# The order of the first ten loads on one queue: projection weights ahead of the tokens

## The chip, the cores and the metric

The kernel runs on one core of one Trainium2 chip. The metric is the device time of one execution in microseconds (us), the median of several executions; lower is better. Five engines run their own instruction streams side by side: PE (matrix products), ACT (ScalarE), DVE (VectorE), POOL (GpSimd) and SP (SyncE), which here issues every transfer. Transfers run on 16 DMA engines that are fed from one queue.

## The reference

The inputs are 2048 tokens `x` of 448 features, the weights `wqkv` (448 x 1344), `wo`, an MLP (`w1`, `b1`, `w2`, `b2`, hidden size 1792) and a gate vector. Two branches are mixed per token:

```
qkv = x @ wqkv                         # 16 heads of 28
o   = softmax(q . k[t - 2 j], j = 0..7) . v[t - 2 j]     # 8 earlier tokens, two apart, masked below 0
a   = o @ wo
b   = relu(x @ w1 + b1)**2 @ w2 + b2
g   = sigmoid(x . gate_w)
out = g * a + (1 - g) * b
```

All inputs are float32.

## The kernel before, in words

Each float32 operand is split into two parts, a high part (a rounded copy, made by ACT: `activation(..., Copy)` into a tile of type float32r) and a low part (the rest, made by DVE: `tensor_sub(raw, high)`). Each product is then three matmuls: high with high, high with low, low with high. PE has nearly all of the work, and everything else is laid beside it.

The 2048 tokens are four chunks of 512 (`CH`), transposed beforehand on the host so that features lie on partitions. The 448 features make four row tiles: `k` = 0, 1, 2 of 128 rows and `k` = 3 of 64 rows, which is stored twice so that it fills 128 partitions. The weights `wqkv` lie in the same row tiles, three blocks of 448 columns (query, key, value); the query block carries two more columns for the gate (450 columns, `NQ`).

The program opens with 13 matmuls on zeros (line 628) and then loads the first chunk and the query weights, which is the part that the change touches (lines 631 to 640). `raws[0]` is the raw query weight tile (`wqraw` in the profile), `rx` the raw tokens of chunk 0 (`xraw`). SP issues in this order, one DMA each, all on the same queue:

| place | before | KB | line |
|---|---|---|---|
| 1 | weights, row tile 0 (w0) | 225 | L635 |
| 2 | tokens, row tile 0, columns 0 to 255 (x0a) | 128 | L640 |
| 3 | tokens, row tile 0, columns 256 to 511 (x0b) | 128 | L640 |
| 4 | weights, row tile 1 (w1) | 225 | L635 |
| 5 | tokens, row tile 1 (x1) | 256 | L640 |
| 6 | weights, row tile 2 (w2) | 225 | L635 |
| 7 | tokens, row tile 2 (x2) | 256 | L640 |
| 8, 9 | weights, row tile 3, two halves of 64 rows (w3a, w3b) | 112.5 each | L638 |
| 10 | tokens, row tile 3 (x3) | 256 | L640 |

Behind them on the queue come the key and value weights (L645, six loads, and L648) and the tokens of chunk 1 (L561, one load of 1024 KB, which reuses the buffer of the query weights).

The splits follow in the loop over `k` from line 650. For each row tile ACT makes the high part of the weights (L651, `wqh`) and then of the tokens in two halves of 256 columns (L658; the very first half is made by DVE, L656). DVE makes the low parts (L659 weights, L661 tokens). ACT and DVE work strictly in program order, so a copy that waits for its load holds back all copies behind it. Row tile 3 is split at L113 and L114 (`w7h`, `w7l`), and so are the key and value weights.

PE's first real work is `qkv_first` (line 249): for `k` = 0, 1, 2 it runs twelve matmuls of 450 columns (L258): four token tiles of 128, three products each, first the two token tiles of columns 0 to 255, then those of 256 to 511. Then row tile 3 and the key weights follow as pairs of matmuls over 64 rows (L187). From there to the end PE works through the other chunks, the MLP (`h` and `b`) and the output projection (`a`). The order on every engine is written out by hand with a planned clock (`advance`, `at`, `when`), which the change does not touch.

Of the kernel before, what the change touches and what calls it, by code (L numbers as in the profile page):

```python
# [14 lines left out]
P = 128  # L15
# [7 lines left out]
CH = 512  # L23
NQ = D + 2
# [32 lines left out]
def gated_mix_kernel(ctx: ExitStack, tc: tile.TileContext, xT, wqkv, w1, w2, wo, b1, b2, out):  # L57
    nc = tc.nc
# [436 lines left out]
    def raw_tile(name):  # L495
        return rawp.tile([P, 4, 512], F32, tag="raw", name=name)
# [133 lines left out]

    raws = [raw_tile("wqraw0")]
    rx = raw_tile("xraw0")
    for k in range(4):
        if k < 3:
            nc.sync.dma_start(raws[0][:, k, :NQ], wqkv[0, :, k])  # L635
        else:
            for b, rows in ((0, slice(0, 64)), (1, slice(64, P))):
                nc.sync.dma_start(raws[0][rows, k, :NQ], wqkv[b, rows, k])  # L638
        for cols in ((slice(0, 256), slice(256, CH)) if k == 0 else (slice(0, CH),)):
            nc.sync.dma_start(rx[:, k, cols], xT[0, :, k, cols])  # L640

    for b, tag in ((1, "k"), (2, "v")):
        raw = attp.tile([P, 3, D], F32, tag=tag, name=f"wqraw{b}")
# [525 lines left out]
```

## Time and profile before

| | |
|---|---|
| time, median of 3 executions | 414.52 us (414.49 to 414.63) |
| the profiled execution's own time | 414.51 us |
| its span in the profile | 412.7 us |
| PE busy in the span | 408.2 us (99%) |
| DVE, ACT, POOL busy | 255.7, 211.3, 268.5 us |
| moved by DMA | 73.76 MB |

All starts are counted in us from the start of the span; 1.8 us of the execution's own time lie outside the span. A timeline row has the start, the time from there to the end of the last instruction in the row, the engine, the line, the operation, what it writes and reads, and in square brackets how long the engine was idle before and what ended that. "SPq" is a DMA being issued, not being moved. "DMA to landing" counts from the issue.

### The profile page before, as it was taken

What the parts mean: (1) busy time and instruction counts of PE and PEld (TensorE: products, weight loads), DVE (VectorE), ACT (ScalarE), POOL (GpSimd) and SP (SyncE); (2) the same over time, 40 slices, a digit from 0 to 9 for tenths busy, and PEclk for the clock granted to TensorE, in tenths of its full rate; (3) what the DMA queues carried; (4) which work ended last, traced back from release to release, by engine and by line L of the source; (5) the groups of instructions that cost most, each with busy time, mean ns of one, the idle gap of its engine ahead of it and who ended that gap; (6) DMA issues with size and microseconds to landing.
All of it is one profiled execution on the core that took longest, in us unless ns stands there. A gap on an engine that the chain in (4) does not pass through costs nothing.

```text
span 412.7 us, 9327 instructions
## 1 busy us (share of the span) xinstructions
PE 408.2 (99%) x3835; PEld 378.0 (92%) x3835; DVE 255.7 (62%) x404; ACT 211.3 (51%) x477; POOL 268.5 (65%) x167
## 2 busy tenths in 40 slices
PE   8999999999999999999999999999999999999997
PEld 7999999999999999888888888989898888888996
DVE  4520433276767766777656798879576677891354
ACT  4641656388765565444565535444653254346540
POOL 0000001955999999989989899999899977940000
DMA  7989999969362315555112649764146630168304
GB/s 226 380 324 326 268 393 299 335 213 311 101 235 104 128 42 218 209 184 152 29 58 95 228 160 270 197 146 149 27 163 186 229 129 2 45 177 132 96 0 180
DMA packets 65611, 73.76 MB, mean 179 GB/s; under 512 B 32352, under 2 KB 58528, under 8 KB 65184
## 3 DMA queue, kind: packets, MB, share of 16 engines
q1 hardware_dynamic: 65568, 73.16, 55.1%
q8 instruction: 30, 0.49, 0.5%
q14 instruction: 13, 0.11, 0.1%
HBM read 45.71 MB, written 28.25 MB: 179 GB/s over the span
## 4 chain that ended last, share of the span: by engine, by line
PE 97%; DMA 1%; SPq 0%; DVE 0%; ACT 0%; issue 0%
PE b L187 33%; PE h L187 32%; PE qkv L187 23%; PE a L187 7%; PE qkv L258 1%; DMA xraw<-xT 1%; PE a L943 1%; PE last L943 0%; SPq L640 0%; SPq L635 0%; DVE bt L822 0%; ACT x L658 0%; PE last L935 0%; PE a L935 0%
## 5 line engine op out<-in xcount | busy, mean ns | idle before, releaser
L334 POOL TENSOR_TENSOR qk<-q,k 128x896 f32<-128x896 f32 x64 | 135.1, 2137 | 84.8 <-DMA k<-k_d 76.4
L341 POOL TENSOR_TENSOR av<-lg,v 128x896 f32<-128x896 f32 x64 | 119.4, 1961 | 6.3 <-DVE lg L335 5.8
L187 PE MATMUL qkv<-wqh,x 64*128 64x448 f32 (+1 forms) x528 | 89.1, 361 | 0.0
L615 DVE TENSOR_TENSOR h<-h,h 128x512 fp32r<-128x512 f32 x56 | 38.4, 688 | 65.9 <-ACT h L618 65.5
L187 PEld LDWEIGHTS qkv<-wqh,x 64*128 64x128 f32 x528 | 72.2, 184 | 0.8
L187 PE MATMUL qkv<-wql,x 64*128 64x448 f32 (+1 forms) x264 | 72.2, 360 | 0.0
L187 PE MATMUL b<-w2ah,h 64*128 64x448 f32 x448 | 68.5, 359 | 0.0
L187 PE MATMUL b<-w2bh,h 64*128 64x448 f32 x448 | 67.8, 360 | 0.0
L335 DVE TENSOR_REDUCE lg<-qk 128x32 f32<-128x896 f32 x64 | 67.0, 1074 | 0.0
L349 DVE TENSOR_REDUCE o<-av 128x112 f32<-128x896 f32 x64 | 66.4, 1070 | 0.1
L616 ACT ACTIVATE h<-h,b1z 128x512 f32<-128x512 f32 x56 | 36.7, 655 | 43.6 <-PE h L187 43.6
L187 PEld LDWEIGHTS b<-w2ah,h 64*128 64x128 f32 x448 | 46.9, 184 | 2.8
L187 PEld LDWEIGHTS b<-w2bh,h 64*128 64x128 f32 x448 | 45.3, 184 | 3.2 <-ACT h L567 0.3
L187 PEld LDWEIGHTS qkv<-wql,x 64*128 64x128 f32 x264 | 44.5, 184 | 0.4
L187 PE MATMUL b<-w2al,h 64*128 64x448 f32 x224 | 44.3, 358 | 0.0
L187 PE MATMUL b<-w2bl,h 64*128 64x448 f32 x224 | 43.2, 358 | 0.0
L206 ACT ACTIVATE st<-qkv 128x448 f32<-128x448 f32 x48 | 24.3, 546 | 34.8 <-PE qkv L187 26.9
L617 ACT ACTIVATE h<-h 128x512 fp32r<-128x512 f32 x56 | 33.5, 598 | 1.7
L618 ACT ACTIVATE h<-h 128x512 f32<-128x512 f32 x56 | 33.3, 594 | 0.0
L187 PE MATMUL h<-x,w1h 64*128 64x512 f32 x168 | 32.8, 386 | 0.0
L567 ACT ACTIVATE h<-h 128x4 fp32r<-128x4 f32 (+1 forms) x35 | 7.2, 207 | 43.1 <-PE b L187 43.0
L187 PE MATMUL h<-x2b,w1h 64*128 64x512 f32 x168 | 28.2, 386 | 0.0
(145 smaller groups left out, 728.7 us busy)
## 6 DMA issues: line engine op xcount, KB each, us to landing
k<-k_d SPq DMA_DIRECT2D x8, 840.0 KB, 6.4
v<-v_d SPq DMA_DIRECT2D x8, 840.0 KB, 4.8
x_d<-x SPq DMA_DIRECT2D x11, 512.0 KB, 6.6
q_d<-st SPq DMA_DIRECT2D x8, 448.0 KB, 4.1
k_d<-st SPq DMA_DIRECT2D x8, 448.0 KB, 4.6
v_d<-st SPq DMA_DIRECT2D x8, 448.0 KB, 5.9
w1raw<-w SPq DMA_DIRECT2D x4, 896.0 KB, 9.2
q<-q_d SPq DMA_DIRECT2D x8, 448.0 KB, 3.6
```

The costliest lines, as they stand in the source:

```text
L187: nc.tensor.matmul(acc.pt[:, :acc.n], a[rows], w[rows], start=acc.todo == acc.all, stop=acc.todo == 1)
L206: nc.scalar.activation(st[:, :, t % 2], pt[:, :D].rearrange("p (g c) -> p g c", g=G), AF.Copy)
L258: nc.tensor.matmul(acc.pt[:, :NQ], a, w, start=k == j == 0, stop=False)
L334: nc.gpsimd.tensor_mul(pr, q[:, s:s + 1].to_broadcast([P, W, C]), k[:, s:s + W])
L335: pending.append(lambda: nc.vector.tensor_reduce(lg[:, s], pr.rearrange("p w (h d) -> p w h d", h=HG), axis=AX.X, op=ALU.add))
L341: nc.gpsimd.tensor_mul(pr.rearrange("p (h d) w -> p w h d", h=HG), lg[:, s][:, :, :, None].to_broadcast([P, W, HG, DH]), v[:, s:s + W].rea ...
L349: nc.vector.tensor_reduce(o[:, g * C:(g + 1) * C], pr, axis=AX.X, op=ALU.add)
L567: nc.scalar.activation(ap, f32(ap), AF.Copy)
L615: nc.vector.tensor_sub(hl, pt, f32(hh))
L616: ops += [lambda pt=pt, r=r: nc.scalar.activation(pt, pt, AF.Relu, bias=b1t[:, f + r:f + r + 1]), lambda pt=pt, hh=hh: nc.scalar.activatio ...
L617: lambda pt=pt, hh=hh: nc.scalar.activation(hh, pt, AF.Square),
L618: lambda pt=pt, r=r, low=low: (nc.scalar.activation(pt, pt, AF.Square), at(delays[r], low))]
```

## The change

The ten loads are put in another order. The weights of each row tile are issued ahead of the (rest of the) tokens of the row tile before it. The sizes of the loads, the tiles they fill, and every instruction of PE, ACT, DVE and POOL and their order stay as they are.

| place | before | after |
|---|---|---|
| 1 | w0 | w0 |
| 2 | x0a | x0a |
| 3 | x0b | w1 |
| 4 | w1 | x0b |
| 5 | x1 | w2 |
| 6 | w2 | x1 |
| 7, 8 | x2, w3a | w3a, w3b |
| 9 | w3b | x2 |
| 10 | x3 | x3 |

```diff
-    for k in range(4):
+    rxf, xf = rx.rearrange("p k n -> p (k n)"), xT[0].rearrange("p k n -> p (k n)")
+
+    def w_raw(k):
         if k < 3:
             nc.sync.dma_start(raws[0][:, k, :NQ], wqkv[0, :, k])
-        else:
-            for b, rows in ((0, slice(0, 64)), (1, slice(64, P))):
-                nc.sync.dma_start(raws[0][rows, k, :NQ], wqkv[b, rows, k])
-        for cols in ((slice(0, 256), slice(256, CH)) if k == 0 else (slice(0, CH),)):
-            nc.sync.dma_start(rx[:, k, cols], xT[0, :, k, cols])
+            return
+        for b, rows in ((0, slice(0, 64)), (1, slice(64, P))):
+            nc.sync.dma_start(raws[0][rows, k, :NQ], wqkv[b, rows, k])
+
+    def x_raw(lo, hi):
+        nc.sync.dma_start(rxf[:, lo:hi], xf[:, lo:hi])
+
+    w_raw(0)
+    x_raw(0, 256)
+    w_raw(1)
+    x_raw(256, 512)
+    w_raw(2)
+    x_raw(512, 1024)
+    w_raw(3)
+    x_raw(1024, 1536)
+    x_raw(1536, 4 * CH)
```

## The prediction

> **What bounds the kernel now.** I read the page first, then the chain of waits, then the timeline of the first 12 us by engine, because the change touches only loads that are issued there.
>
> ```profile
> span 412.7 us, 9327 instructions
> PE 408.2 (99%) x3835; PEld 378.0 (92%) x3835; DVE 255.7 (62%) x404; ACT 211.3 (51%) x477; POOL 268.5 (65%) x167
> PE 97%; DMA 1%; SPq 0%; DVE 0%; ACT 0%; issue 0%
> ```
>
> PE is busy for 408.2 of 412.7 us and makes 97% of the chain that ended last. So the end of the kernel is the moment at which PE can start without a break, plus a fixed amount of PE work. The chain, in order of time, tells where that moment is, and the waits of PE over the whole span whether there is another one:
>
> ```profile
> 2.60 4.59 DMA xraw<-xT
> ...
> 7.22 0.42 ACT x L658
> ...
> 7.69 5.09 PE qkv L258 x24
> 12.78 12.28 PE qkv L187 x117
> ```
>
> ```profile
> PE qkv L258 <- ACT x L658: 0.3, 1, 0.3
> ```
>
> The load issued at 2.60 is x1, the tokens of row tile 1. It lands at 2.60 + 4.59 = 7.19; ACT copies its first half from 7.22 on; PE starts row tile 1 at 7.69 and from there is never short of work. (PE's one wait after its warm-up is shown as 0.3 us because the ends of matmuls are modelled.) From landing to PE it is 7.69 - 7.19 = 0.50 us. Whatever moves x1's landing moves the end by the same amount, in either direction, until another step is later.
>
> How the landings follow one another is seen in ACT's timeline, where a copy that waited begins when its load has landed:
>
> ```profile
> 3.45 0.58 ACT L651 ACTIVATE wqh<-wqraw 128x450 fp32r<-128x450 f32 x1 [1.42 <-DMA wqraw<-wqkv]
> 5.42 0.42 ACT L658 ACTIVATE x<-xraw 128x256 fp32r<-128x256 f32 x1 [1.39 <-DMA xraw<-xT]
> 6.05 0.58 ACT L651 ACTIVATE wqh<-wqraw 128x450 fp32r<-128x450 f32 x1 [0.21 <-DMA wqraw<-wqkv]
> 7.22 0.72 ACT L658 ACTIVATE x<-xraw 128x256 fp32r<-128x256 f32 x2 [0.59 <-DMA xraw<-xT]
> 7.88 0.58 ACT L651 ACTIVATE wqh<-wqraw 128x450 fp32r<-128x450 f32 x1
> 9.22 0.72 ACT L658 ACTIVATE x<-xraw 128x256 fp32r<-128x256 f32 x2 [0.76 <-DMA xraw<-xT]
> 10.04 0.58 ACT L113 ACTIVATE w7h<-wqraw 128x450 fp32r<-128x450 f32 x1
> 10.57 0.63 ACT L113 ACTIVATE x<-xraw 128x512 fp32r<-128x512 f32 x1
> ```
>
> These are w0, x0b, w1, x1, w2, x2, row tile 3 of the weights, x3: the landings come in the order of issue. Before x1's copy ACT sat idle for 0.59 us with w1 already copied. The weights of row tile 1 are therefore not what row tile 1 waits for; its tokens are.
>
> Issue is no limit. SP issues the ten loads by 5.27 + 0.58 us, while most land later than 5:
>
> ```profile
> 2.13 0.43 SPq L635 DMA_DIRECT2D wqraw<-wqkv  x1
> 2.60 0.43 SPq L640 DMA_DIRECT2D xraw<-xT  x1
> 3.08 0.43 SPq L635 DMA_DIRECT2D wqraw<-wqkv  x1
> 3.55 0.43 SPq L640 DMA_DIRECT2D xraw<-xT  x1
> 4.03 1.20 SPq L638 DMA_DIRECT2D wqraw<-wqkv  x2
> 5.27 0.58 SPq L640 DMA_DIRECT2D xraw<-xT  x1
> ```
>
> The busy time by stretches (last two columns: share of the DMA engines, GB/s) says what is the limit:
>
> ```profile
> 3.25:4.25 1.00, 1.00 (x7) 0.91 (x5) 0.48 (x2) 0.58 (x1) 0.00 (x0) 1.00 0.56 117
> 4.25:7.25 3.00, 3.00 (x13) 2.36 (x12) 1.79 (x4) 1.03 (x3) 0.00 (x0) 1.00 1.00 303
> 7.25:10.00 2.75, 2.43 (x12) 2.17 (x12) 1.76 (x5) 1.94 (x5) 0.00 (x0) 1.00 1.00 299
> ```
>
> From 4.25 on the transfers run at some 300 GB/s with all engines busy: the queue is worked off in order and a load lands when the bytes ahead of it are through. Before that there is a dip of about 1 us at 117 GB/s, just behind the first two loads.
>
> **The change part by part.** No instruction of PE, ACT, DVE or POOL changes or changes place; ten loads of the same sizes keep one queue. Only landings move.
>
> *x1 goes from fifth to sixth place; w2 (225 KB) goes ahead of it.* By bytes: 225 x 1024 = 230,400 bytes at 303 GB/s are 0.76 us. By a row: x1 will have ahead of it and in it exactly the set of loads that w2 had before (w0, x0a, x0b, w1, x1, w2). The landing times by line give w2's:
>
> ```profile
> L635 SPq DMA_DIRECT2D wqraw<-wqkv x3: 390/432/432, 0.7 to 3.1; - x3
> DMA to landing us min/median/max: 2.7/3.7/4.8
> ```
>
> The longest of the three is w2's: 3.08 + 4.8 = 7.88, the moment at which ACT copied it. So x1 lands at 7.88 instead of 7.19, 0.69 us later. Against that stands the dip. It held 111 packets in 1 us:
>
> ```profile
> DMA packets 111, 0.12 MB, mean 117 GB/s; under 512 B 8, under 2 KB 111, under 8 KB 111
> ```
>
> 0.12 MB in 111 packets are 1.08 KB each, so these were mostly x0b's rows of 1024 bytes, and few of w1's of 1800. Now w1 comes first there. If the dip lets through so many packets and not so many bytes, each packet carries up to 776 bytes more: at most 111 x 776 = 86 KB, or 0.28 us at 303 GB/s. This bounds the term between 0.76 - 0.28 = 0.48 and 0.76 us. I take 0.65, near the row for the same set of loads, with a little of the dip won back. The Trainium skill ("DMA: Bandwidth & Descriptors", Specifications) gives about 358 GB/s per core from HBM and 435 for the fabric; w2 would by those take 0.64 or 0.53 us, and the sum would be 415.15 or 415.04; the trace's 303 and 299 GB/s stand below both.
>
> *x0b goes behind w1.* It now lands when w1 did before (same set of loads): 2.13 + 3.7 = 5.83, or 6.05 by ACT's row, instead of 5.42. PE's second six matmuls of row tile 0 start about 0.5 us later. At 5.09 / 24 = 0.21 us each they need 1.3 us and end by about 7.8. PE then has to wait for x1 until 7.19 + 0.65 + 0.50 = 8.34 anyway. Cost nothing; the cover is x1's own delay, and without it the cost would be the same 0.5 us. ACT copies w1 behind x0b's half (0.42 + 0.58 us) and is done by 7.1, before x1.
>
> *x2 goes behind both halves of w3.* It lands when w3b did (all loads but x3):
>
> ```profile
> L638 SPq DMA_DIRECT2D wqraw<-wqkv x2: 567/576/586, 4.0 to 4.6; - x2
> DMA to landing us min/median/max: 5.4/5.5/5.6
> ```
>
> 4.6 + 5.4 gives 10.0 instead of 9.22. Its copy of 0.42 us makes row tile 2 ready for PE at about 10.5. PE wants it when the twelve matmuls of row tile 1 are through: half of the 5.09 us for 24, 2.54 us after 8.34, at 10.9. It is hidden, with 0.4 us left (before: 10.23 against about 9.7).
>
> *x3, w3, w2.* w2 and w3 land earlier and nobody waited for them. x3 keeps its place and has landed by 10.57. ACT comes to it after x2's copies, w7 and itself: 10.0 + 0.72 + 0.58 + 0.63 = 11.9; PE needs row tile 3 at 10.9 + 2.54 = 13.4. Nothing.
>
> *Queues behind.* The weights' buffer is read last by the split of row tile 3, now some 0.7 us later, and chunk 1's tokens reuse it:
>
> ```profile
> 11.31 0.33 SPq L561 DMA_DIRECT2D xraw<-xT  x1
> 23.57 2.19 ACT L113 ACTIVATE x<-xraw 128x512 fp32r<-128x512 f32 x4
> ```
>
> ```profile
> DMA to landing us min/median/max: 6.9/7.0/7.9
> ```
>
> That load is issued at 12.0 instead of 11.31 and lands at 20 at the latest with the longest landing time of its line (7.9 us); it is used at 23.57. Nothing. All stores behind it wait for PE's results and shift with PE.
>
> *Sum.* +0.65 us on the profiled execution's 414.51: 415.16. The median of the runs is 414.52, the same within 0.01, so 415.2. That is 0.16%. What a measurement of this kernel tells from no change is about 0.2%, 0.83 us here, so I forecast "within", on the slow side.
>
> **The rivals.**
>
> *The slowest DMA engine lags at x1's new place.* A load has landed when the last of 16 engines has written its share. x2 landed at 9.22, 1.34 us behind w2, though 256 KB take 0.87 us at 303 GB/s: 0.47 us of lag at that place. If x1, now the load before x2's old place, catches that lag, it lands at 7.88 + 0.47 = 8.35: +1.16 us, 415.7, slower. It decides from a lag of 0.14 us (7.88 to 8.02) on. For it: lag of this size is in the rows, and x2 comes next with only 0.4 us left. Against it: w2 itself landed at this place without it.
>
> *The dip belongs to x0b and goes.* With 303 instead of 117 GB/s in that microsecond 186 KB more are through, 0.61 us: +0.08 us, 414.6, not slower. For it: mostly x0b's rows moved in it. Against it: x0a's rows had the same size and went through without a dip, so the dip looks like one of the start. For faster by 0.83 us x1 would have to land by 7.19 - 0.83 = 6.36, with 225 KB more ahead of it than now; I see no way to it but a queue that isn't worked off in order.
>
> *PE's clock falls back in the longer pause.* PE started slowly and doubled its pace:
>
> ```profile
> 4.17 1.09 PE L258 MATMUL qkv<-wqh,x 128*128 128x450 f32 x2
> ...
> 5.05 0.64 PE L258 MATMUL qkv<-wql,x 128*128 128x450 f32 x2
> ...
> 8.21 0.58 PE L258 MATMUL qkv<-wql,x 128*128 128x450 f32 x2
> 8.62 0.96 PE L258 MATMUL qkv<-wqh,x 128*128 128x450 f32 x4
> ```
>
> Two matmuls took 5.05 - 4.17 = 0.88 us, later 8.62 - 8.21 = 0.41 us. If the pauses around 6.2 and 8 us slowed the next twelve, that is 12 x (0.44 - 0.20) = 2.9 us: 418.1 with the delay. Against it: the pause before 7.69 did no such thing, and the new one is about twice as long. The Trainium skill ("TensorE: Matmul & The Clock Gate", Part 1) lets the clock fall after an idle window of about 3.4 us, which would leave it up here.
>
> **How the numbers follow.** Forecast 0.56; lag 0.31; dip gone 0.08; clock 0.02; some way to a gain over 0.2% 0.03. Within 0.2% are the forecast and the dip: 0.64. Slower are lag and clock: 0.33. Faster 0.03. The range runs from the dip's 414.6 to the lag's 415.7 and leaves out the clock, the gain and the tails of the lag.
>
> **What would show it.** Right: in the profile after, x1's ACT copy (the one before PE's long run) begins at 7.7 to 8.0 after a wait for its load, PE's row tile 1 at 8.2 to 8.5, x0b's at 5.8 to 6.1, and from row tile 1 on every PE row is later by one constant. The dip is there again behind the second load. Wrong: x1 lands by 7.3 (the dip was x0b's), or after 8.02, or row tile 2 makes PE wait a second time (x2 after 10.4), or matmuls of 450 columns are 0.4 us apart beyond 8 us.

## The result, and the profile after

| | before | after |
|---|---|---|
| time, median (lowest to highest) of 19 runs each | 414.52 us (413.93 to 414.99) | 415.24 us (414.91 to 415.72) |
| the profiled execution's own time | 414.51 us | 415.39 us |
| its span | 412.7 us | 413.5 us |

The ratio of the runs, after to before, is 1.0020 with a 95% interval of 1.0013 to 1.0026: a small loss, 0.72 us between the medians, and the interval excludes "no change". The forecast was 415.2.

The page after has the same shape, PE carries the same share of the chain, and only the span is longer:

```profile
span 413.5 us, 9327 instructions
PE 408.1 (99%) x3835; PEld 377.9 (91%) x3835; DVE 255.5 (62%) x404; ACT 211.1 (51%) x477; POOL 268.6 (65%) x167
PE 97%; DMA 1%; SPq 1%; DVE 0%; ACT 0%; issue 0%
```

The chain of the first 25 us (start, length, what) has the same links as before, each later:

```profile
3.08 4.98 DMA xraw<-xT
...
8.08 0.42 ACT x L672
...
8.55 5.09 PE qkv L258 x24
13.64 11.41 PE qkv L187 x108
```

x1 is issued at 3.08, one place later, and lands at 3.08 + 4.98 = 8.06 instead of 7.19. PE begins row tile 1 at 8.55 instead of 7.69 and row tile 3 at 13.64 instead of 12.78: 0.86 us later in both rows. PE's waits now show two places where there was one, and PE's timeline says which:

```profile
PE qkv L258 <- ACT x L672: 1.1, 2, 0.6
```

```profile
5.42 0.58 PE L258 MATMUL qkv<-wqh,x 128*128 128x450 f32 x2
6.60 0.68 PE L258 MATMUL qkv<-wqh,x 128*128 128x450 f32 x2 [0.60 <-ACT x L672]
7.12 0.56 PE L258 MATMUL qkv<-wql,x 128*128 128x450 f32 x2
7.52 0.56 PE L258 MATMUL qkv<-wqh,x 128*128 128x450 f32 x2
8.55 0.69 PE L258 MATMUL qkv<-wqh,x 128*128 128x450 f32 x2 [0.46 <-ACT x L672]
9.07 0.57 PE L258 MATMUL qkv<-wql,x 128*128 128x450 f32 x2
```

The first wait is for x0b, the second for x1. The six matmuls behind the first end at 7.52 + 0.56 = 8.08 and x1 is ready at 8.55, so the first wait costs nothing: had it been shorter, PE would have waited longer for x1. ACT's timeline gives the landings, to be read against the eight rows of before:

```profile
6.13 0.42 ACT L672 ACTIVATE x<-xraw 128x256 fp32r<-128x256 f32 x1 [2.10 <-DMA xraw<-xT]
6.46 0.56 ACT L665 ACTIVATE wqh<-wqraw 128x450 fp32r<-128x450 f32 x1
8.08 0.72 ACT L672 ACTIVATE x<-xraw 128x256 fp32r<-128x256 f32 x2 [1.06 <-DMA xraw<-xT]
8.71 0.56 ACT L665 ACTIVATE wqh<-wqraw 128x450 fp32r<-128x450 f32 x1
9.59 0.72 ACT L672 ACTIVATE x<-xraw 128x256 fp32r<-128x256 f32 x2 [0.32 <-DMA xraw<-xT]
```

The copies of w1 and w2 now start without a wait: these weights are early. From x0b on all waiting is for tokens, and that for x1 has grown from 0.59 to 1.06 us.

### The profile page after: what moved, and what is told of

Read it like the earlier page. It is cut to its first block, busy times and chain, and to the rows that moved or that the text cites. A ratio compares the mean times of both kernels' runs of the same rounds, so it can differ in the third digit from the quotient of the medians.

```text
span 413.5 us, 9327 instructions
## 1 busy us (share of the span) xinstructions
PE 408.1 (99%) x3835; PEld 377.9 (91%) x3835; DVE 255.5 (62%) x404; ACT 211.1 (51%) x477; POOL 268.6 (65%) x167
## 4 chain that ended last, share of the span: by engine, by line
PE 97%; DMA 1%; SPq 1%; DVE 0%; ACT 0%; issue 0%
PE b L187 33%; PE h L187 32%; PE qkv L187 23%; PE a L187 7%; PE qkv L258 1%; DMA xraw<-xT 1%; PE a L957 1%; SPq L637 0%; PE last L957 0%; SPq L643 0%; DVE bt L836 0%; ACT x L672 0%; PE last L949 0%; PE a L949 0%
## 5 line engine op out<-in xcount | busy, mean ns | idle before, releaser
L187 PE MATMUL qkv<-wqh,x 64*128 64x448 f32 (+1 forms) x528 | 89.1, 361 | 0.0
L187 PEld LDWEIGHTS qkv<-wqh,x 64*128 64x128 f32 x528 | 71.9, 184 | 0.8
L187 PE MATMUL qkv<-wql,x 64*128 64x448 f32 (+1 forms) x264 | 72.0, 360 | 0.0
L187 PE MATMUL b<-w2ah,h 64*128 64x448 f32 x448 | 68.3, 359 | 0.0
L187 PE MATMUL b<-w2bh,h 64*128 64x448 f32 x448 | 67.7, 360 | 0.0
L187 PEld LDWEIGHTS b<-w2ah,h 64*128 64x128 f32 x448 | 46.5, 184 | 2.8
L187 PEld LDWEIGHTS b<-w2bh,h 64*128 64x128 f32 x448 | 45.1, 184 | 3.2 <-ACT h L567 0.3
L187 PEld LDWEIGHTS qkv<-wql,x 64*128 64x128 f32 x264 | 44.3, 184 | 0.4
L187 PE MATMUL b<-w2al,h 64*128 64x448 f32 x224 | 44.0, 358 | 0.0
L187 PE MATMUL b<-w2bl,h 64*128 64x448 f32 x224 | 42.9, 358 | 0.0
L187 PE MATMUL h<-x,w1h 64*128 64x512 f32 x168 | 32.6, 386 | 0.0
L187 PE MATMUL h<-x0b,w1h 64*128 64x512 f32 x168 | 28.1, 386 | 0.0
```

The lines of the kernel that those rows point to most:

```text
L187: nc.tensor.matmul(acc.pt[:, :acc.n], a[rows], w[rows], start=acc.todo == acc.all, stop=acc.todo == 1)
```

## The experiments

All edits are to the order or the cut of the ten loads (one adds matmuls at the start). Diffs are against the calls of the changed kernel. Ratios are to the kernel before, run on the same chip beside each, with 95% intervals.

**Theory:** the end is set by x1's landing, and that by the bytes ahead of x1 on the queue. **Rivals:** x0b's or x2's new place costs it; or the landings scatter with the slowest DMA engine and the order matters little.

### One move at a time

x0b and w1 alone change places:

```diff
     w_raw(1)
     x_raw(256, 512)
-    w_raw(2)
     x_raw(512, 1024)
-    w_raw(3)
+    w_raw(2)
     x_raw(1024, 1536)
+    w_raw(3)
     x_raw(1536, 4 * CH)
```

> Only x0b and w1 change places (w0, x0a, w1, x0b, x1, w2, x2, w3a, w3b, x3). Theory (the time is set by x1's landing, and that by the bytes ahead of it on the queue): x1 has the same 706 KB ahead of it as before, x0b's delay is covered by x1's; within 0.2 us of before, 414.3 to 414.7. Rival (x0b behind w1 is what costs, since PE's second half of row tile 0 starts late): about +0.5 to +0.8 us. Rival (the slowest DMA engine lags at random places): no pattern, anything within 0.5 us.

Measured: 414.72 us against 414.41, ratio 1.0006 (0.9997 to 1.0015). The interval holds no change, but it also reaches to 0.6 us, so by itself it does not shut out the first rival's lower end; its middle is 0.3 us. In its chain no load appears any more; from the matmuls on zeros on, it is PE alone:

```profile
1.19 3.14 PE warm L628 x13
4.34 8.43 PE qkv L258 x36
12.77 12.28 PE qkv L187 x117
```

PE reaches row tile 3 at 12.77, as before (12.78), though nothing waits: x1 was copied from 6.92 on, and PE was just that slow. Why is told with PE's pace, in the last section.

x1 and w2 alone change places:

```diff
-    w_raw(1)
     x_raw(256, 512)
+    w_raw(1)
     w_raw(2)
     x_raw(512, 1024)
-    w_raw(3)
     x_raw(1024, 1536)
+    w_raw(3)
     x_raw(1536, 4 * CH)
```

> Only x1 and w2 change places (w0, x0a, x0b, w1, w2, x1, x2, w3a, w3b, x3). Theory: x1 has w2's 225 KB more ahead of it and lands where w2 did, 7.8 to 8.1 instead of 7.2; +0.6 to +0.9 us, the whole of the change's cost. Rival (x0b's place costs): no change, within 0.2 us of before.

Measured: 415.14 us, ratio 1.0015 (1.0006 to 1.0024): this move alone is slower than before beyond its interval, and the 0.73 us between the medians (0.25 to 1.0 by the interval) are as much as the whole change's cost. Its profiled execution landed x1 earlier than forecast, at 7.54:

```profile
3.08 4.46 DMA xraw<-xT
...
7.56 0.42 ACT x L672
...
8.03 5.09 PE qkv L258 x24
13.11 12.01 PE qkv L187 x114
```

So x1 with the same loads ahead of it, though w1 and x0b stand the other way round, landed at 8.06 in one execution and at 7.54 in another. The different order need not be the reason: in the two profiles of one kernel, x1 in halves below, ACT's copy of x0b began at 5.98 and at 5.62, and over the seven profiles in which x0b follows w0 and x0a it began between 4.99 (x1 ahead of w1) and 6.35 (the second dose). Landings scatter by some tenths up to a microsecond and more, and medians of many runs are needed to see the cost: the spans of the 12 executions with x1 alone have a median of 413.25 us, those of the 35 of before run beside them 412.6, while this profile's 413.0 shows only part of the loss.

x2 and w3 alone change places:

```diff
-    w_raw(1)
     x_raw(256, 512)
-    w_raw(2)
+    w_raw(1)
     x_raw(512, 1024)
+    w_raw(2)
     w_raw(3)
     x_raw(1024, 1536)
```

> Only x2 and the two halves of w3 change places (w0, x0a, x0b, w1, x1, w2, w3a, w3b, x2, x3). Theory: x2 lands about 10.0 instead of 9.2, PE wants row tile 2 at 10.2 and its copy ends at about 10.4 to 10.5: at the edge of the slack, 0 to +0.3 us. Rival (x2 is what costs): +0.6 us or more, with a second wait of PE at row tile 2.

Measured: 414.62 us, ratio 1.0003 (0.9993 to 1.0012). ACT's copy of x2 began at 9.47, when it had landed, and PE did not wait at row tile 2. It is hidden; the interval allows for at most 0.5 us.

### A second dose

```diff
-    w_raw(1)
     x_raw(256, 512)
+    w_raw(1)
     w_raw(2)
+    w_raw(3)
     x_raw(512, 1024)
-    w_raw(3)
     x_raw(1024, 1536)
```

> A second dose: w2 and both halves of w3, 450 KB, are issued ahead of x1 (w0, x0a, x0b, w1, w2, w3a, w3b, x1, x2, x3). Theory (bytes ahead of x1): at 303 GB/s x1 lands about 1.5 us later than before, 8.5 to 8.9; PE starts row tile 1 at 9.0 to 9.4; +1.2 to +1.7 us, twice the cost of w2 alone. Rival (one place later on the queue is lost in the scatter of the slowest engine): +0.5 to +0.9, no more than with w2 alone.

Measured: 416.61 us against 414.40, ratio 1.0073 (1.0051 to 1.0095). Twice the bytes cost more than twice the time: 2.2 us, where 1.2 to 1.7 were expected. (Two of its six executions took 418.84 and 419.05 us, the other four 416.28 to 416.67; the two have no profile.) The chain still goes through x1, which lands at 4.32 + 4.90 = 9.22, 2.03 us later than before:

```profile
4.32 4.90 DMA xraw<-xT
...
9.24 0.42 ACT x L672
...
9.71 5.09 PE qkv L258 x24
14.80 10.21 PE qkv L187 x96
```

The transfers were slower here: the stretch from 3.25 to 4.25 moved 90 GB/s against 117 before, that from 4.25 to 7.25 266 against 303, together some 0.14 MB less, which are about 0.5 us at these rates. That is the part beyond the price of the 450 KB; why they were slower stays open. The rival that a place is lost in the scatter falls: both doses move the end, and the larger one moves it more.

### The opposite order

```diff
-    w_raw(1)
     x_raw(256, 512)
-    w_raw(2)
     x_raw(512, 1024)
-    w_raw(3)
+    w_raw(1)
+    w_raw(2)
     x_raw(1024, 1536)
+    w_raw(3)
```

> The opposite of the change for row tile 1: x1 is issued ahead of w1 (w0, x0a, x0b, x1, w1, w2, x2, w3a, w3b, x3). Theory: both are needed and the last of them lands at 7.2 as before, but it is now w1, and ACT copies w1 (0.58) and then x1's half (0.42) behind that landing instead of x1's half alone: PE's row tile 1 starts at 8.2 to 8.3; +0.5 to +0.6 us. Rival (only x1's landing counts): -0.4 us or more.

Measured: 415.49 us, ratio 1.0027 (1.0016 to 1.0037). The direction is the theory's, the size twice the expected: w1 takes x1's place in the chain, and ACT's two copies follow on its landing,

```profile
2.60 5.46 DMA wqraw<-wqkv
...
8.08 0.58 ACT wqh L665
8.66 0.32 ACT x L672
...
9.02 5.08 PE qkv L258 x24
```

but w1 landed at 8.06, not at 7.2, although the loads up to its end are the same five as those up to x1's end before. In this profile PE's row tile 3 starts 1.32 us later than before: 0.46 of them are the longer way from landing to PE (9.02 - 8.06 = 0.96 instead of 0.50 us), which is what the theory priced, and 0.87 are the later landing, which it had put at nothing. So ACT's copy of the weights does cost when they come behind the tokens of their own row tile; before, it hid behind the tokens' landing. In none of these orders did more lead than that buy anything.

### Smaller and larger loads

x1 as two loads of 256 columns, in the order of before:

```diff
     x_raw(0, 256)
+    x_raw(256, 512)
     w_raw(1)
-    x_raw(256, 512)
+    x_raw(512, 768)
+    x_raw(768, 1024)
     w_raw(2)
-    x_raw(512, 1024)
+    x_raw(1024, 1536)
     w_raw(3)
-    x_raw(1024, 1536)
```

> The order of before, but x1 is loaded as two halves of 256 columns, one DMA each. Theory: the first half has 128 KB less in it, lands 0.42 us earlier at 303 GB/s (about 6.8), PE starts row tile 1 at about 7.3 and does not wait again (second half at 7.7, row tile 2 at 9.8 with x2's copy done by 9.7): -0.3 to -0.45 us, 414.1. Rival (the wait is not for bytes but for the slowest engine or the number of loads): no change, or slower by the extra load's issue of 0.43 us.

Measured: 414.38 us, ratio 0.9991 (0.9979 to 1.0003), unclear. I ran it once more:

> The order of before with x1 as two loads, once more, for its interval: if it is better than before by the 0.09% of its first runs, both sets of runs lie below 1; if x0b's landing (6.0 in its profile) takes the place of x1's as the bound, it stays within 0.1% of before.

Measured: 414.57 us against 414.54, ratio 1.0000 (0.9991 to 1.0009). No measurable gain. In the first profile the chain goes through x0b instead, which landed at 5.96 with nothing changed ahead of it:

```profile
1.66 4.30 DMA xraw<-xT
...
5.98 0.42 ACT x L673
...
6.45 6.29 PE qkv L258 x30
12.74 12.28 PE qkv L187 x117
```

In the second profile no load is in the chain, only PE itself from the matmuls on zeros on, and row tile 3 starts at 12.90. So x0b, x1 and PE's own pace from its first matmul lie close together at the bound in the order of before; taking one away shows the next.

x0 as one load, alone and with x1 in halves:

```diff
-    x_raw(0, 256)
+    x_raw(0, 512)
     w_raw(1)
-    x_raw(256, 512)
+    x_raw(512, 1024)
     w_raw(2)
-    x_raw(512, 1024)
-    w_raw(3)
     x_raw(1024, 1536)
+    w_raw(3)
```

> The order of before, but x0 is one load of 256 KB (w0, x0, w1, x1, w2, x2, w3a, w3b, x3). Theory A (the dip comes behind the second load whatever it holds): x0b is through before the dip, the dip falls on w1; PE starts row tile 0 about 0.4 us later (4.5 to 4.8) but never waits for x0b, and x1 lands 0.2 to 0.4 us earlier; -0.2 to -0.4 us. Theory B (the dip belongs to x0b's rows or to bytes): x1 lands at 7.2 as before and the later start of PE costs nothing; within 0.15 us of before.

> x0 as one load and x1 as two halves (w0, x0, w1, x1a, x1b, w2, x2, w3a, w3b, x3). Theory: with x0b's wait gone the earlier landing of x1's first half can show: PE's row tile 1 starts at 7.1 to 7.3 and the floor is PE's own work from its first matmul on; -0.3 to -0.6 us. Rival: PE's own work from its first matmul on is the bound already in the kernel before; no change, or slower by PE's later start of 0.4 us.

The second cuts x1 in halves as above besides. Measured: 417.13 us, ratio 1.0067 (1.0055 to 1.0079), and 416.63 us, ratio 1.0047 (1.0032 to 1.0062). All my theories for these two failed. The dip (the slow stretch from 3.25 to 4.25 us) did not wait for the second load to end; x0 fell into it and landed at 5.4 (4.95 in the second kernel), where x0a had landed at 3.7. PE, which had run out of zeros to multiply at 4.3, paused, and then ran slowly (the first kernel of the two):

```profile
5.84 1.09 PE L258 MATMUL qkv<-wqh,x 128*128 128x450 f32 x2 [1.50 <-ACT x L671]
6.73 0.95 PE L258 MATMUL qkv<-wql,x 128*128 128x450 f32 x2
7.48 1.70 PE L258 MATMUL qkv<-wqh,x 128*128 128x450 f32 x4
```

Two matmuls take 6.73 - 5.84 = 0.89 and 7.48 - 6.73 = 0.75 us; ten of them ran at this pace, where others have 0.2 us each. To tell the pace from the late data, the first of the two with more matmuls on zeros (the only edit against it):

```diff
-WARM = 13
+WARM = 22
```

> x0 as one load, as in the kernel whose PE waited 1.5 us for it and then ran its first ten matmuls at 0.37 us each; the only other edit is 22 matmuls on zeros at the start instead of 13, so that PE has something to do until x0 lands at 5.4. Theory (that kernel's loss is PE's clock, which rises late because of the pause): the first matmuls of row tile 0 are 0.2 us apart soon after they start, and the time falls by 1 to 1.9 us from 417.1, to 415.2 to 416.1. Rival (its loss is the late landing of x0 and x1 alone): no change, 416.9 to 417.3.

Measured: 415.71 us, ratio 1.0029 (1.0018 to 1.0040): 1.2 us above its own before, where 13 matmuls gave 2.7, and 1.4 us between the two medians, which are from two chips (0.9 between the two profiled executions). The loads came no earlier (x0 at 5.39 again); PE's pace rose after four matmuls instead of ten:

```profile
6.05 0.95 PE L258 MATMUL qkv<-wqh,x 128*128 128x450 f32 x2
6.80 0.84 PE L258 MATMUL qkv<-wql,x 128*128 128x450 f32 x2
7.47 0.77 PE L258 MATMUL qkv<-wqh,x 128*128 128x450 f32 x3
```

So about half of the 2.7 us was the slow pace after the pause. The rest I have not split further: the data are late, the zeros now last until 6.25 where PE could have begun at 5.84, and four matmuls still ran slowly. None of these versions beats the kernel before.

### One number behind all of them

PE's start of row tile 3 (the chain's first L187) against the span:

| kernel | row tile 3 starts | span | difference |
|---|---|---|---|
| before | 12.78 | 412.7 | 399.9 |
| after | 13.64 | 413.5 | 399.9 |
| x0b alone | 12.77 | 412.8 | 400.0 |
| x1 alone | 13.11 | 413.0 | 399.9 |
| x2 alone | 12.62 | 412.5 | 399.9 |
| x1 in halves | 12.74 | 412.7 | 400.0 |
| w2 and w3 ahead | 14.80 | 414.7 | 399.9 |
| x0 whole | 15.16 | 415.1 | 399.9 |
| x0 whole, x1 in halves | 15.27 | 415.3 | 400.0 |
| x0 whole, 22 matmuls | 14.28 | 414.2 | 399.9 |
| x1 ahead of w1 | 14.10 | 413.9 | 399.8 |

In these eleven profiles, whatever the loads do, the end is this start plus 399.9 us, within 0.1. The twelfth, the second one of x1 in halves, is the exception told last.

## Why the prediction was right, point by point

- **The end moves with x1's landing, one to one.** Shown for this change: x1's landing is 0.87 us later, PE's starts go from 7.69 to 8.55 and from 12.78 to 13.64, and the table carries that on to the end. In the other direction it holds for almost nothing: with x1 in halves the next bound is there at once.
- **The term for x1, 0.65 us (0.48 to 0.76).** 0.72 us between the medians, 0.73 with x1's move alone; both inside. The profiled execution missed the marks I had set, each a little on the late side: x1's copy at 8.08 (7.7 to 8.0), PE's row tile 1 at 8.55 (8.2 to 8.5), x0b's copy at 6.13 (5.8 to 6.1), and x1's landing at 8.06 is beyond the 8.02 that I had called a sign of being wrong. That execution was 0.15 us above its median; by the table's rule the median one had x1 at about 7.9, an estimate. I had treated the lag as another case with a chance of 0.31; it is a spread on the forecast's own term, in both directions. That the middle came within 0.07 us is in part luck: the same counting of bytes gave 0.5 to 0.6 where 1.1 us was measured (x1 ahead of w1), 1.2 to 1.7 where it was 2.2 (second dose), and a gain where there was none (x1 in halves).
- **"A load lands when the bytes ahead of it are through."** Only roughly. From the start of the span to x1's landing, in the profile before and then after:

```profile
DMA packets 940, 1.37 MB, mean 190 GB/s; under 512 B 98, under 2 KB 737, under 8 KB 940
DMA packets 1111, 1.62 MB, mean 201 GB/s; under 512 B 130, under 2 KB 898, under 8 KB 1111
```

  The loads up to and with x1 are only 0.99 and 1.22 MB: in both some 0.4 MB of the loads behind it had moved too. So the queue is not worked off load by load, and the price of w2's bytes held while this overlap stayed the same (0.36 MB with x1 alone and with the second dose). With x1 ahead of w1 it was 0.6 MB when w1 landed, and with x0 whole 0.7 MB when x1 did: there the landings came 0.9 and some 1.5 us later than the count of bytes says. What makes the overlap grow stays open. That ACT copied w2 at 7.88 did not confirm w2's landing either, for ACT was at x1's copies until then.
- **The dip is one of the start, not of x0b.** Right. With x0b third, as before, but x1 ahead of w1 the stretch from 3.25 to 4.25 moved 178 GB/s, so its rate does not hang on w1's longer rows alone. After, it moved 144 GB/s in fewer and larger packets: 27 KB more than before, 0.09 us at 303 GB/s, were won back, about what the working took:

```profile
DMA packets 92, 0.14 MB, mean 144 GB/s; under 512 B 7, under 2 KB 92, under 8 KB 92
3.25:4.25 1.00, 1.00 (x6) 0.79 (x4) 0.28 (x2) 0.58 (x1) 0.00 (x0) 1.00 0.76 144
```

- **x0b's delay costs nothing while x1 is later still.** Right in the kernel after (8.08 against 8.55). Alone it may cost up to 0.15% by its interval, and its landing, forecast for 5.83 to 6.05, came just before its copy at 6.13.
- **x2 behind w3 is hidden.** Right; its copy began at 9.59, earlier than the 10.0 of the working, and PE did not wait.
- **PE's clock does not fall in the pauses.** Right; from 8.55 on the 24 matmuls of the chain take 5.09 us, 0.21 each as before. The rival's price of 0.44 us a matmul was too high, because it held the slow start of the first one: a slow matmul in a row of them takes 0.37. But the last experiments show that the rival was no idle thought: a pause of 1.5 us before the pace has risen costs about 1.4 us.
- **Within 0.2%.** 0.17% by the medians, 0.20% by the ratio of the runs. The bound was set too wide for this kernel: with 19 runs a side the interval begins at 0.13%, so the loss is real. The sum was right; calling it "within" says only that it is small.

## What to carry to other kernels

Where one queue is full, putting a load ahead delays what it passes, here by about the time of its bytes or more; ask first which load the waiting engine lacks. Here it was the tokens, so weights were the wrong thing to advance; as far as these orders show, they need only as much lead as their own copy takes. And a start-up stage has several bounds close together (x0b, x1, PE's own pace), so a repair of one is worth no more than the distance to the next.

## What the runs showed of the hardware that I had not expected

**The dip at the start.** In all twelve profiles the transfers ran at 258 to 321 GB/s from 2.5 to 3.25 us, then at 90 to 181 from 3.25 to 4.25, then at 264 to 334 from 4.25 to 7.25, whether the third load was x0b or w1 and whether the second had 128 or 256 KB. It comes about 1.5 us after the first data (1.75 us), not behind a given load. Its cause stays open.

**PE's pace rises at its own time.** The pace doubled soon after 5 us before, at some 4.7 after, at some 6.4 with x0b alone moved and at 7.2 with 22 matmuls on zeros, although PE had work from 1.2 us on in each; with the pause of 1.5 us at 9.7. With x1 alone moved it was there by about 4.5 already (two matmuls from 4.13 to 4.68). The granted clock of the profile (PEclk) reads 1.00 in all these stretches, slow or fast, so the pace is read from the matmuls' own rows. In the kernels before and after PE waited for x1 behind the rise, so it did not set their ends; it is why PE alone filled the time up to 12.77 when x0b alone was moved. The Trainium skill ("TensorE: Matmul & The Clock Gate", Part 1) has a free-running window of about 3.4 us that must be busy from end to end, so that the rise comes at a phase that varies between runs. By an estimate from the page's window the earliest and latest rise would be 4.6 and 8.0 us here, with a start at 1.2. The 4.5 to 7.2 us of these profiles agree within 0.1. Each slow matmul of 450 columns costs 0.17 us more (0.37 against 0.2), so where PE is the bound this alone can make runs differ by some tenths.

**A rare loss at 70 us.** The second profile with x1 in halves has a span of 414.1 with row tile 3 at 12.90, 1.3 us more than the table's rule. DVE's timeline shows four small subtractions, 64 x 64, that took 8.59 us together, where the first profile of that kernel has 1.29 (the second profile's row, then the first's):

```profile
69.06 8.59 DVE L114 TENSOR_TENSOR w17l<-w1raw,w17h 64x64 fp32r<-64x64 f32 x4 [0.94 <-ACT w17h L113]
```

```profile
68.90 1.29 DVE L114 TENSOR_TENSOR w17l<-w1raw,w17h 64x64 fp32r<-64x64 f32 x4 [0.94 <-ACT w17h L113]
```

POOL's timelines show what stood beside them, again in the second and in the first:

```profile
69.01 8.49 POOL L334 TENSOR_TENSOR qk<-q,k 128x896 f32<-128x896 f32 x4 [67.62 <-DMA k<-k_d]
```

```profile
71.24 8.41 POOL L334 TENSOR_TENSOR qk<-q,k 128x896 f32<-128x896 f32 x4 [69.86 <-DMA k<-k_d]
```

POOL's multiplications, released by the attention's first keys, began 0.05 us before DVE's subtractions; each subtraction then took as long as one POOL multiplication (2.13 us) and PE waited 1.0 us, up to 77.79. In the first profile POOL started at 71.24, behind the subtractions. In the profile with 22 matmuls on zeros DVE began first, at 70.44, and POOL at 71.44; there the four subtractions took 3.27 us and PE did not wait. In the other ten profiles they took 1.28 or 1.29 us. So they are slow where they overlap POOL, whichever starts first. The Trainium skill ("SBUF — State Buffer", Who interferes with whom) describes the port pair that DVE and GpSimd share as an exclusive lock and says that a DVE instruction with two SBUF inputs contends with a GpSimd instruction that reads SBUF; the rows agree. Two executions of the kernel before, 416.03 and 416.77 us, may have lost their time in the same way; they have no profile.
